# The order of two GpSimd remainders in the attention stage of a fused attention and mixture-of-experts kernel

## The chip, the cores and the metric

The kernel runs on one core of a Trainium2 chip. The metric is the device time of one execution in microseconds (us). The engines have the names of the profile: PE is TensorE's matrix multiply and PEld its weight load, DVE is VectorE, ACT is ScalarE, POOL is GpSimd, SP is SyncE, which here only issues DMAs. "SPq" is SP's queue of DMA issues.

## The reference, cut to what matters

```python
# attention: batch 4, 8 heads, 576 positions, head width 64, all float32
scores = scale * np.matmul(q, k.transpose(0, 1, 3, 2))          # scale = 1/8
cum = np.cumsum(np.log(np.clip(f, 0.0001, 1.0)), axis=-1)
scores = np.where(causal, -1e9, scores + cum[:, :, :, None] - cum[:, :, None, :])
attn = softmax(scores)                                          # over the last axis
x = np.matmul(attn, v)                                          # -> (2304, 512)
# then a layer of 8 experts (top 1, 512 -> 1024 -> 512), then a maxout layer of
# three 512x768 products and a 768x512 output product
```

The change touches only how q and k are prepared for the product of q and k.

## The kernel before, in words

Attention comes first and takes the first 222 us or so of the span; the routing and the experts follow, and then the shared layer. The 32 heads are worked on as 16 pairs of heads (p = 0 to 15, head h = 2p or 2p + 1), four pairs to a batch.

The product of q and k is made with matrix multiplies on a rounded 32-bit type (fp32r), so each operand is split in two: a high part, which is the operand cast to fp32r, and a low part, the remainder operand minus high part. For each pair there are four steps in `split_tasks(p)`:

- `q_hi` casts q into the tile At (128 partitions x 1152 elements, by DVE at L433 or by ACT at L435, both in the helper `evict`), and `k_hi` casts k into R1 the same way. The profile calls R1 and R2 both "R".
- `q_lo` (L321) computes the remainder of q on GpSimd, 64 x 1152 elements, into the other half of At; `k_lo` (L324) does the same for k, into R2.
- `q_copy` (L327) is a DMA that SP issues: it copies the cast q into the tile Bt.
- `load_pair` (L251) loads q and k of a pair as four DMAs, first two for q, then two for k, and `load_decay` (L262) loads two rows of the decay. Both are issued by SP. The raw q and k have two buffers each, so the load of pair p + 2 has to wait until all four steps of pair p have read theirs. At, Bt, R1 and R2 have three buffers.

A score task (L344) of a head multiplies At by R1 and Bt by R2 into a PSUM buffer "s" (three of them). DVE then takes the negated and masked maximum out of it (L361, tile P and its maximum nm), which frees the buffer; ACT takes the exponential (L381); PE transposes the result (L393 to L401, tiles t and tl), DVE or ACT copies it into PT (L433, L435), PE multiplies by v (L459, po), DVE or ACT copies that out (ot), PE turns it back (L478, pb), DVE scales it into XL (L487), and SP stores it (L498). At the end of a batch DVE does the routing of the batch's tokens (`route_batch`, with L550, L686 and L724 among its operands and steps).

The order of the instructions on each engine is fixed when the kernel is built, by a planner (`Sched`). A task has a list of engines that may do it, a planned cost for each, a number that says how urgent it is (smaller is earlier), and tasks that it waits for. The planner keeps a clock for each engine, takes again and again the open task that can start first (among equals the more urgent), gives it to the engine on which it would end first, with a handicap of 0.15 us for DVE and 2.0 us for GpSimd, and adds 0.2 us (`HOP`) where the task it waits for was on another engine. The tasks of pair p have the number 10 p - 6; the softmax tasks of head h have numbers from 5 h on. The planner knows of no case in which one engine slows another.

Of the kernel before, what the change touches and what calls it, by code (L numbers as in the profile page):

```python
# [214 lines left out]
def attention(tc, g, qT, kT, v, x_dram, es):  # L215
# [30 lines left out]
    def load_pair(p):  # L246
        q2 = ld.tile([128, 2, S], F32, tag="q2", name=f"q2_{p}")
        k2 = ld.tile([128, 2, S], F32, tag="k2", name=f"k2_{p}")
        for t, src in ((q2, qT), (k2, kT)):
            for r in range(2):  # L250
                nc.sync.dma_start(out=t[64 * r:64 * r + 64], in_=src[p])  # L251
        raws[p] = q2, k2
# [7 lines left out]
    def load_decay(p):  # L260
        for r, c in enumerate((g.chi, g.clo)):
            nc.sync.dma_start(out=R2[p % NQ][64 + r:65 + r].bitcast(F32).rearrange("p r s -> p (r s)"),  # L262
                              in_=c[2 * p:2 * p + 2, :].bitcast(F32))
# [28 lines left out]
    sd = Sched({"s": 3, "P": NPB, "t": 2, "tl": 1, "o": 2, "ot": 2}, 11.0)  # L292
# [11 lines left out]
    def split_tasks(p):  # L304
        i, u = p % NQ, 10 * p - 6
        load = None
        if p > 1:
            old = [fs[h, t, k] for h in (2 * p - 6, 2 * p - 5) for t in range(NBLK) for k in range(1 + (t == 4))] if p >= NQ else []
            load = sd.task("SP", 3.3, lambda e: load_pair(p), u - 8, ready[p - 2], lat=2.0)
            dec = sd.task("SP", 1.3, lambda e: load_decay(p), u - 4, old, lat=2.0)  # L310
        else:
            old, dec = [], None

        def q_hi(e):
            evict(e, At[i], raws[p][0])

        def k_hi(e):
            evict(e, R1[i], raws[p][1])

        def q_lo(e):  # L320
            nc.gpsimd.tensor_tensor(out=At[i][64:128], in0=raws[p][0][64:128], in1=At[i][64:128].bitcast(F32), op=ALU.subtract)  # L321

        def k_lo(e):
            nc.gpsimd.tensor_tensor(out=R2[i][0:64], in0=raws[p][1][0:64], in1=R1[i][0:64].bitcast(F32), op=ALU.subtract)  # L324

        def q_copy(e):
            nc.sync.dma_start(out=Bt[i][0:64].bitcast(F32), in_=At[i][0:64].bitcast(F32))  # L327

        qh = sd.task(("ACT", "DVE"), (1.02, 0.67), q_hi, u, old + [load])
        ql = sd.task("Pool", 2.6, q_lo, u, [qh])  # L330
        qc = sd.task("SP", 0.9, q_copy, u, [qh], lat=2.0)
        kh = sd.task(("ACT", "DVE"), (1.02, 0.67), k_hi, u, old + [load])
        kl = sd.task("Pool", 2.6, k_lo, u, [kh])
        ready[p] = [x for x in (qh, ql, qc, kh, kl, dec) if x is not None]

    def s_task(h, t, k, j0, w):
# [94 lines left out]
    def evict(e, out, in_):  # L431
        if e == "DVE":
            nc.vector.tensor_copy(out, in_)  # L433
        else:
            nc.scalar.activation(out=out, in_=in_, func=AF.Copy)  # L435
# [71 lines left out]

    last = [None]
    split_tasks(1)
    for p in range(NP):  # L510
        b, hp = divmod(p, NPAIR)
        if p + 2 < NP:
            split_tasks(p + 2) if p + 2 > 1 else None
        if hp == 1 and b + 1 < B:
            vdep[b + 1] = sd.task("SP", 3.3, lambda e, b=b: load_v(b + 1), 40 * b + 20, [fo[NPAIR * b - 1, u] for u in range(2)] if b else [], lat=2.0)
        head(2 * p)
        head(2 * p + 1)
        pair_out(p)
        if hp == NPAIR - 1:
            batch_out(b)  # L520
# [939 lines left out]
```

## Time and profile before

| what | value |
|---|---|
| median of 3 runs | 785.78 us (785.52 to 785.88) |
| the profiled execution | 785.06 us, of which its span 783.3 us and 1.76 us around it |
| mean granted clock of TensorE | 0.984 of full speed |
| PE busy | 738.9 us, 94% of the span |
| DVE busy | 461.9 us, 59% |
| ACT busy | 368.2 us, 47% |
| POOL busy | 237.7 us, 30% |

A share of busy time is a mean over stages with different limits; the change lies in the attention stage alone, so its stretches are what is to be read. An instruction that is held up after it has begun counts as busy for all of that time. A wait is put down to what was released last by the record, and "issue" is time in which the record shows nothing that was waited for.

### The profile page before, as it was taken

The page shows a single profiled execution, that of the slowest core. Times are in us where ns is not written, and L with a number is a line of the kernel's source. Part 1 is how long each engine was busy: PE and PEld are TensorE (multiplying, and loading weights), DVE is VectorE, ACT ScalarE, POOL GpSimd, SP SyncE. Part 2 cuts the span into 40 slices and gives each one's busy share as a digit, 9 for nine tenths or more (in the row PEclk, how much of TensorE's full clock was granted, in tenths as well). Part 3 has the DMA queues.
Part 4 walks back from the last instruction along what each step waited for, and adds up shares of the span by engine and source line. Part 5 has one row for each costly group of instructions (what it writes and reads, how often), then busy time and mean ns, then how long its engine had stood idle before and what let it go on. Part 6 is the DMA issues. An engine that isn't in the chain of part 4 may idle for free.

```text
span 783.3 us, 13403 instructions
## 1 busy us (share of the span) xinstructions
PE 738.9 (94%) x4862; PEld 682.3 (87%) x4862; DVE 461.9 (59%) x1076; ACT 368.2 (47%) x870; POOL 237.7 (30%) x189
## 2 busy tenths in 40 slices
PE   2989999999949998999999999999999999999996
PEld 1868877778738998999999999989999899999995
DVE  6888887988567998867767877941211211112110
ACT  5668887978836653454554563231211212212111
POOL 7464443532020344234223113341221211212112
PEclk9999999999978999999999999999999999999998
DMA  9959775751145465556474653200000000100001
GB/s 228 239 125 216 191 178 143 182 118 40 23 116 208 151 220 181 186 181 233 151 257 147 230 198 126 82 28 14 1 40 1 28 14 1 41 0 15 28 1 43
DMA packets 44614, 90.19 MB, mean 115 GB/s; under 512 B 23320, under 2 KB 23320, under 8 KB 44544
## 3 DMA queue, kind: packets, MB, share of 16 engines
q1 hardware_dynamic: 40960, 77.83, 34.0%
q0 software_dynamic: 3152, 9.88, 3.5%
q10 hardware_dynamic: 432, 1.57, 0.5%
q8 instruction: 40, 0.66, 0.3%
q14 instruction: 30, 0.25, 0.1%
HBM read 74.97 MB, written 9.44 MB: 108 GB/s over the span
## 4 chain that ended last, share of the span: by engine, by line
PE 75%; DVE 9%; DMA 7%; issue 4%; ACT 1%; POOL 1%; SPq 1%; POOLq 0%; DVEq 0%; ACTq 0%
PE pm L907 10%; PE pm L906 10%; PE pm L908 10%; PE s L344 6%; PE po L459 6%; PE t L397 4%; PE ph L908 3%; PE ph L907 3%; PE py L906 3%; PE py L908 3%; PE ph L906 3%; PE py L907 3%; PE po L1268 3%; PE po L1267 3%; PE po L1266 3%
## 5 line engine op out<-in xcount | busy, mean ns | idle before, releaser
L1240 DVE TENSOR_TENSOR tm<-pm,tm 128x384 f32<-128x384 f32 x72 | 40.1, 557 | 199.4 <-PE pm L908 198.2
L907 PE MATMUL pm<-x_y,m 128*128 128x384 f32 x432 | 144.5, 335 | 0.0
L908 PE MATMUL pm<-x_y,m 128*128 128x384 f32 x432 | 144.4, 334 | 0.0
L906 PE MATMUL pm<-x_y,m 128*128 128x384 f32 x432 | 144.4, 334 | 0.0
L381 ACT ACTIVATE P<-P,nm 128x576 f32<-128x576 f32 (+4 forms) x160 | 88.3, 555 | 17.0 <-DVE nm L361 16.7
L344 PE MATMUL s<-R,At 128*128 128x192 f32 (+1 forms) x192 | 71.3, 380 | 14.9 <-DVE At L271 10.5
L934 ACT ACTIVATE w<-stg 128x1024 fp32r<-128x1024 f32 x63 | 66.2, 1056 | 33.3 <-DMA stg<-in_w_dram 14.4
L907 PEld LDWEIGHTS pm<-x_y,m 128*128 128x128 f32 x432 | 81.1, 188 | 0.6 <-POOL x_y L1199 0.3
L951 DVE TENSOR_TENSOR w<-stg,w 128x1024 fp32r<-128x1024 f32 x54 | 70.2, 1304 | 19.3 <-ACT w L934 18.9
L907 PE MATMUL ph<-x,w 128*128 128x384 f32 (+7 forms) x256 | 79.3, 310 | 2.1 <-DVE x L1083 2.1
L906 PEld LDWEIGHTS pm<-x_y,m 128*128 128x128 f32 x432 | 81.1, 188 | 0.2
L908 PEld LDWEIGHTS pm<-x_y,m 128*128 128x128 f32 x432 | 81.1, 188 | 0.0
L906 PE MATMUL py<-h,w 128*128 128x384 f32 (+7 forms) x256 | 79.5, 311 | 0.8 <-DVE h L1141 0.8
L908 PE MATMUL ph<-x,w 128*128 128x384 f32 (+7 forms) x256 | 79.4, 310 | 0.8 <-DVE w L951 0.7
L906 PE MATMUL ph<-x,w 128*128 128x384 f32 (+7 forms) x256 | 79.4, 310 | 0.7 <-ACT x L934 0.7
L1251 POOL TENSOR_TENSOR g<-tm,g 128x384 fp32r<-128x384 f32 x34 | 36.5, 1074 | 141.4 <-ACT g L934 141.4
L908 PE MATMUL py<-h,w 128*128 128x384 f32 (+7 forms) x256 | 78.5, 307 | 0.4 <-DVE w L951 0.4
L907 PE MATMUL py<-h,w 128*128 128x384 f32 (+7 forms) x256 | 78.2, 305 | 0.0
L934 ACT ACTIVATE g<-tm 128x384 fp32r<-128x384 f32 x36 | 18.8, 524 | 115.9 <-DVE tm L1240 115.9
L361 DVE CUSTOM_DVE_ANT_0 P<-s,mask 128x288 f32<-128x288 f32 (+4 forms) x160 | 64.4, 422 | 11.1 <-PE s L344 6.7
L344 PE MATMUL s<-R,Bt 66*128 66x192 f32 (+1 forms) x192 | 60.2, 320 | 4.3 <-DMA R<-clo 4.3
L321 POOL TENSOR_TENSOR At<-q,At 64x1152 fp32r<-64x1152 f32 x15 | 40.3, 2684 | 77.1 <-DVE At L433 24.7
(246 smaller groups left out, 1620.4 us busy)
## 6 DMA issues: line engine op xcount, KB each, us to landing
stg<-in_w_dram SPq DMA_DIRECT2D x61, 512.0 KB
q<-in_q_dram SPq DMA_DIRECT2D x32, 288.0 KB
k<-in_k_dram SPq DMA_DIRECT2D x32, 288.0 KB
sd<-in_m_dram SPq DMA_DIRECT2D x18, 512.0 KB
Bt<-At SPq DMA_DIRECT2D x16, 288.0 KB
v<-in_v_dram SPq DMA_DIRECT2D x4, 1024.0 KB
x_dram<-XL SPq DMA_DIRECT2D x64, 64.0 KB
sd_o<-in_mo_dram SPq DMA_DIRECT2D x6, 512.0 KB
```

Source lines behind the costliest of these rows:

```text
L321: nc.gpsimd.tensor_tensor(out=At[i][64:128], in0=raws[p][0][64:128], in1=At[i][64:128].bitcast(F32), op=ALU.subtract)
L344: nc.tensor.matmul(st[:, 0:wp], lt[0:kk, r, ROW0[t]:ROW0[t] + 128], rt[0:kk, r, j0:j0 + wp], start=(ps_i == 0), stop=(ps_i == 1))
L361: nc.vector.tensor_tensor_reduce(out=P[0:n, j0:j0 + w], in0=st_.pop((h, t, k))[0:n, 0:w], in1=g.mask[0:n, m0:m0 + w], scale=-0.125, scalar ...
L381: nc.scalar.activation(out=P[0:n, 0:ext], in_=P[0:n, 0:ext], func=AF.Exp, bias=nm[0:n, k:k + 1], scale=-1.0, accum_out=sums[b][0:n, t, h % ...
L459: nc.tensor.matmul(po[64 * r:64 * r + 64, lo - c0:w], vt[b][0:n, a, (2 * hp + r) * D:(2 * hp + r + 1) * D], PT[(2 * p + r) % NPT][0:n, a, ...
L906: nc.tensor.matmul(out, whi, xhi, start=start, stop=False)
L907: nc.tensor.matmul(out, whi, xlo, start=False, stop=False)
L908: nc.tensor.matmul(out, wlo, xhi, start=False, stop=stop)
L934: nc.scalar.activation(out=out, in_=in_, func=AF.Copy)
L951: ENG[e].tensor_tensor(out=w[:, 1], in0=t, in1=w[:, 0].bitcast(F32), op=ALU.subtract)
L1240: nc.vector.tensor_tensor(out=mx[0], in0=mx["p", w][:, 0:MC], in1=mx[0], op=ALU.max)
L1251: ENG[e].tensor_tensor(out=ht[:, 1, :], in0=mx[0], in1=ht[:, 0, :].bitcast(F32), op=ALU.subtract)
```

## The change

In the kernel before, the cast of k does not depend on that of q, the remainder of q is given to GpSimd when the cast of q is done, and the remainder of k when the cast of k is done. After the change the cast of k depends on the cast of q, the remainder of k depends on the cast of k as before, and the remainder of q depends on the cast of q and on the remainder of k. So GpSimd gets the remainder of k first. The planned costs of the cast of k go from 1.02 to 1.1 us on ACT and from 0.67 to 0.8 us on DVE. The list `ready[p]`, which the score tasks and the load of pair p + 2 wait for, holds the same tasks.

```diff
         qh = sd.task(("ACT", "DVE"), (1.02, 0.67), q_hi, u, old + [load])
-        ql = sd.task("Pool", 2.6, q_lo, u, [qh])
         qc = sd.task("SP", 0.9, q_copy, u, [qh], lat=2.0)
-        kh = sd.task(("ACT", "DVE"), (1.02, 0.67), k_hi, u, old + [load])
+        kh = sd.task(("ACT", "DVE"), (1.1, 0.8), k_hi, u, old + [load, qh])
         kl = sd.task("Pool", 2.6, k_lo, u, [kh])
+        ql = sd.task("Pool", 2.6, q_lo, u, [qh, kl])
         ready[p] = [x for x in (qh, ql, qc, kh, kl, dec) if x is not None]
```

Pair 0 is split by code outside the planner (`first_split`) that the change leaves alone, so 15 pairs are affected.

## Rows read from the trace of the kernel before

**Rows 1.** The page's first part: busy time, share of the span and instructions.

```profile
PE 738.9 (94%) x4862; PEld 682.3 (87%) x4862; DVE 461.9 (59%) x1076; ACT 368.2 (47%) x870; POOL 237.7 (30%) x189
```

**Rows 2.** Stretches: length; busy PE, PEld, DVE, ACT, POOL; PE clock, DMA share, GB/s.

```profile
45.20:47.60 2.40, 0.02 (x2) 0.00 (x1) 2.40 (x6) 0.16 (x1) 1.65 (x2) 1.00 0.15 32
47.60:51.10 3.50, 3.50 (x15) 2.77 (x15) 2.35 (x11) 2.01 (x5) 3.42 (x2) 0.51 1.01 248
51.10:104.00 52.90, 52.90 (x439) 43.40 (x438) 45.66 (x157) 45.77 (x149) 24.47 (x10) 1.00 0.77 185
104.00:118.00 14.00, 12.32 (x97) 9.58 (x96) 12.32 (x40) 11.06 (x39) 6.21 (x4) 1.00 0.89 196
```

**Rows 3.** PE's timeline, idle places (one like 105.16 left out): in brackets idle time, releaser.

```profile
47.60 0.46 PE L344 MATMUL s<-R,At 128*128 128x192 f32 x1 [2.38 <-DVE nm L361]
...
105.16 0.41 PE L344 MATMUL s<-R,At 128*128 128x320 f32 x1 [0.84 <-DVE nm L361]
...
117.73 1.00 PE L478 MATMUL pb<-w,ot 128*128 128x144 f32 x6 [0.83 <-DVE ot L433]
...
167.37 1.00 PE L478 MATMUL pb<-w,ot 128*128 128x144 f32 x6 [0.87 <-DVE ot L433]
```

**Rows 4.** The chain that ended last, 97 to 118 us: start, length, what.

```profile
103.23 1.66 issue
...
115.01 1.96 DVE R L433
```

**Rows 5.** DVE's groups of instructions, 16 to 222 us: busy, mean ns, idle before.

```profile
L433 DVE CAST R<-k 128x1152 fp32r<-128x1152 f32 x13 | 26.5, 2036 | 0.0
...
L433 DVE CAST At<-q 128x1152 fp32r<-128x1152 f32 x12 | 10.9, 911 | 0.0
...
L724 DVE TENSOR_TENSOR ohp<-iota,rm 128x640 f16<-128x640 f32 x3 | 2.5, 826 | 0.0
```

**Rows 6.** DVE's timeline, single instructions: start, length.

```profile
29.60 0.64 DVE L550 TENSOR_TENSOR tri<-ioe,iok 128x64 f32<-128x64 f32 x1
...
40.25 2.50 DVE L433 CAST R<-k 128x1152 fp32r<-128x1152 f32 x1
...
43.51 2.63 DVE L433 CAST At<-q 128x1152 fp32r<-128x1152 f32 x1
46.06 0.75 DVE L433 CAST R<-k 128x1152 fp32r<-128x1152 f32 x1
...
101.89 3.07 DVE L433 CAST R<-k 128x1152 fp32r<-128x1152 f32 x1
...
125.92 0.76 DVE L433 CAST At<-q 128x1152 fp32r<-128x1152 f32 x1
```

**Rows 7.** POOL's timeline, single instructions: start, length, idle before.

```profile
27.53 2.64 POOL L321 TENSOR_TENSOR At<-q,At 64x1152 fp32r<-64x1152 f32 x1 [4.46 <-issue]
30.24 2.64 POOL L324 TENSOR_TENSOR R<-k,R 64x1152 fp32r<-64x1152 f32 x1
39.50 2.63 POOL L321 TENSOR_TENSOR At<-q,At 64x1152 fp32r<-64x1152 f32 x1 [6.62 <-DVE nm L361]
42.89 2.63 POOL L324 TENSOR_TENSOR R<-k,R 64x1152 fp32r<-64x1152 f32 x1 [0.75 <-DVE R L433]
46.27 3.04 POOL L321 TENSOR_TENSOR At<-q,At 64x1152 fp32r<-64x1152 f32 x1 [0.75 <-issue]
...
101.71 2.64 POOL L321 TENSOR_TENSOR At<-q,At 64x1152 fp32r<-64x1152 f32 x1 [2.42 <-DVE At L433]
```

**Rows 8.** The instructions of tile At: duration ns min/median/max, first and last start.

```profile
L435 ACT ACTIVATE At<-q x3: 1154/1156/1163, 11.4 to 142.2; 128x1152 fp32r<-128x1152 f32 x3
```

**Rows 9.** PE's timeline: the first score matmul of pair 2.

```profile
36.84 0.30 PE L344 MATMUL s<-R,At 128*128 128x288 f32 x1
```

**Rows 10.** SP's timeline: the four load issues of one pair.

```profile
104.38 1.11 SPq L251 DMA_DIRECT2D q<-in_q_dram  x2
107.76 1.10 SPq L251 DMA_DIRECT2D k<-in_k_dram  x2
```

## The prediction

> **What bounds the kernel now.** I read the page's first part, then the stretches of the attention stage, then the idle places of PE and the chain through them, and last the timelines of DVE and POOL side by side. The page says that PE is busy for 94% of the span [rows 1]. In the attention stage it is the bound almost without a break: in the stretch from 51.1 to 104.0 us it is busy for all of the 52.9 us, while DVE has 45.66 and ACT 45.77 us of work [rows 2]. So what a change here is worth is what it does to the moments in which PE stands still. From 30 us to the end of the score matmuls there are five: 2.38 us before 47.60, and 0.84, 0.83, 0.84 and 0.87 us (the third of these, before 154.79, repeats that before 105.16 to the hundredth) [rows 3]. Together they are 5.76 us. The first costs more than its length: PE was granted its full clock up to it, and in the 3.5 us behind it the clock was 0.51 of full speed, the lower of its two levels [rows 2]. At full speed that work would have taken 3.5 x 0.51 = 1.79 us, so 1.71 us more were lost. After the shorter gaps the clock did not fall: the stretch that holds those at 105.16 and 117.73 shows 1.00 [rows 2]. All five therefore cost 5.76 + 1.71 = 7.47 us.
>
> The releaser of each gap is DVE [rows 3]: nm of the softmax's first step, or the copy ot. What made DVE late is the instruction in front of these. The chain has the cast of k for 1.96 us just ahead of the gap at 117.73 [rows 4]. Ahead of 105.16 it has 1.66 us of "issue" [rows 4], which is a hole in the record of waits and not a cause: DVE's timeline shows a cast of k from 101.89 to 104.96 there [rows 6]. In front of the first gap stand two such casts in a row, 2.50 us from 40.25 and 2.63 us from 43.51 [rows 6].
>
> Those casts are held up. A cast that is left alone takes 0.75 us (the one at 46.06 [rows 6]). The 13 casts of k on DVE took 26.5 us where 13 x 0.75 = 9.75 would do, and the 12 of q took 10.9 where 9.0 would do [rows 5], so 16.7 + 1.9 = 18.6 us of DVE's time are lost. Put beside POOL, each long one ends some 0.6 us after a POOL subtraction ends. The cast at 40.25 ends at 42.75, the subtraction that began at 39.50 ends at 42.13; the cast at 43.51 ends at 46.14, the subtraction that began at 42.89 ends at 45.52; the one at 101.89 ends at 104.96, the subtraction that began at 101.71 ends at 104.35 [rows 6, 7]. So DVE's cast stands still while POOL subtracts. The Trainium skill says the same in "SBUF — State Buffer", section "Who interferes with whom": the two engines share one pair of ports, whoever starts first has it for its whole instruction, and casts are among the operations that need it. That rule also speaks against part of the change, and I come back to it among the rivals.
>
> **The change part by part.** The remainder of q may no longer start on the cast of q; POOL's first subtraction of a pair now waits for the cast of k, and that waits for the cast of q. So neither cast can meet a subtraction of its own pair. Ten or so casts of k were held by their own pair's `q_lo`, and all of the 16.7 us belongs to them; the 1.9 us belong to one cast of q, that at 43.51, which was held by the `k_lo` of the pair before.
>
> *The four later gaps.* Each stands behind one cast of k held by its own pair (3.07 us at 101.89, excess 2.3; the others have the same pattern). The excess is larger than the gap, so the gap goes whole: 0.84 + 0.83 + 0.84 + 0.87 = 3.38 us. A gap that went only in part would leave something between 0 and 3.38; I take the whole, as DVE has 52.9 - 45.66 = 7 us of slack in 53 us even with its stalls [rows 2].
>
> *The first gap.* The cast of k at 40.25 loses its stall of 2.50 - 0.75 = 1.75 us and ends near 41.0. Then POOL takes the remainder of k until 41.0 + 2.63 = 43.6 and that of q until 46.3. The cast of q of the next pair comes 1.75 us earlier, at 41.8, and still meets POOL. Its cost has two bounds, and nothing at all if the planner's new order puts it elsewhere. If it slips in between the two subtractions it is held to 43.6, 1.8 us, as long as now (1.88). If POOL's second subtraction goes first, it is held to 46.3, 1.8 + 2.63 = 4.4 us, against 3.63 us for both stalls now: 0.8 us worse. No row shows who wins when a cast waits at the seam of two subtractions. The nearest is the cast of k at 46.06, right behind a cast of q: it took 0.75 us, and the subtraction that began beside it at 46.27 ran long, 3.04 in place of 2.63 us [rows 6, 7], so a subtraction does give way to a cast. I take the middle: DVE is 1.75 us less late, the gap shrinks from 2.38 to 0.63 us, shorter than those after which the clock held, so the 1.71 us come back as well: 1.75 + 1.71 = 3.46 us. The bounds are 2.38 + 1.71 = 4.09 gained and 0.8 lost.
>
> *The new waits.* The cast of k behind that of q costs nothing on DVE, which takes them in turn anyway. Where the cast of q is on ACT (3 of 15, 1.156 us each [rows 8]) the cast of k starts up to 1.2 us later. POOL starts a pair's block at the end of the second cast and not of the first, but loses the wait between its two subtractions (0.75 us at 42.89 [rows 7]), so the block ends within about a microsecond of where it did. What waits for the block is the pair's first score matmul. It is nearest for pair 2, where `k_lo` ends at 30.24 + 2.64 = 32.88 and the scores begin at 36.84 [rows 7, 9]. There the cast of k was done by 30.24 at the latest, so the new block ends by 30.24 + 2 x 2.64 = 35.5: hidden by 1.3 us even so. If that cover went, each microsecond would be one of PE.
>
> The load of pair p + 2 starts with q, whose buffer now comes free last. SP issued q at 104.38 and had to wait to 107.76 for k [rows 10]; now it would issue q at about 107.8 and k at 108.9, 1.1 us later, with the stores of XL, the decay rows and `q_copy` queued behind. The cast that needs this load, two pairs on, begins at 125.92 [rows 6], 18 us after the k load was issued, so I cost it at nothing; what would uncover it is a load slower than some 17 us, and then it is the 1.1 us.
>
> *The planned costs* of 0.8 and 1.1 us change only the order. They move the choice between DVE and ACT by 0.05 us; the dependency moves it by 0.2 us towards the engine that did the cast of q, mostly DVE (12 of 15 [rows 5, 8]).
>
> Sum: 3.38 + 3.46 = 6.8 us off the profiled 785.06, so 778.3 us. The median of the runs is 0.72 us above that execution, so 779.0 us. What follows the attention is a separate plan and moves as a block.
>
> **The rivals.**
>
> *The pair 3 to 4 collision is not relieved.* POOL now has its two subtractions back to back, and if the second takes the port first, the first gap gives nothing or loses 0.8 us: 3.38 - 0.8 = 2.6 to 3.4 us gained, 782.4 to 783.2 us. For it speaks that the seam is untried; against it that POOL gave way at 46.06.
>
> *Other DVE work is held instead.* The operation at L550, 64 elements wide, ran from 29.60 to 30.24, to the end of the subtraction that began at 27.53 [rows 6, 7]: it was held too. The routing has a chain of such operations; today they are free of it (L724, ten times as wide, takes 826 ns [rows 5]). If the moved blocks meet two batches' routing, each loses up to one subtraction, 2.6 us, of which PE feels between 0.8 and 2.4 by the gaps in [rows 3]: 1.7 to 4.8 us back, 780.7 to 783.8 us. The Trainium skill has this rule as well ("SBUF — State Buffer", "Who interferes with whom"): a DVE instruction with two inputs in SBUF meets a GpSimd instruction that reads SBUF at the shared port. By that rule the row at L550 is one more case of the hold, and the trace agrees.
>
> *The new order gives it back.* The planner is greedy; a shift of 0.1 us can give the copies and exponentials another engine. PE's 7.5 us could come back as other gaps: 784.3 to 787 us. Against it: outside the casts nothing made PE wait.
>
> *Slower: the cast of k goes to ACT.* There it takes 1.156 us and delays an exponential; ACT is already at 45.77 of 52.9 us. If all 13 moved and each opened a gap of 0.84 us, 10.9 us are lost, net 4.1: 789.9 us. It decides from 6.8 / 13 = 0.52 us a cast. Against it: the 0.2 us for changing engine.
>
> *Slower: pair 2 comes late*, if its cast of k is put off beyond 31.6 us, with a cold clock behind the gap: 6.8 us would need a block over 4 us late, 786 to 789 us.
>
> **How the numbers follow.** The forecast has 0.57, the collision 0.14, the routing 0.06, the given back 0.11, ACT 0.08, pair 2 0.04. Within 0.2%, 1.6 us, a measurement of this kernel hardly tells a difference from none; that is 784.2 to 787.4 us. Faster: 0.57 + 0.14 + 0.06 = 0.77; same 0.11; slower 0.12. The forecast's own range is 777.8 (all 7.5 us and half a microsecond of spread) to 780.7. For 8 in 10 the range takes in the collision, the routing and the edge of the given back: 777.5 to 785.0.
>
> **What would show it.** Right: casts of k on DVE near 0.75 us, their group near 10 us in place of 26.5; no PE gap at the four later places; no stretch near 0.5 clock around 48 us; `k_lo` ahead of `q_lo` on POOL, back to back. Wrong: casts still over 2 us with POOL busy, which would name the collision; new waits of PE for P or PT behind ACT; PE waiting for R or At at a pair's first score.

## The result, and the profile after

The changed kernel takes 777.32 us (median of 4 runs, 776.84 to 778.65) against 785.83 us (4 runs, 785.52 to 786.92): a ratio of 0.990, with a 95% interval of 0.9879 to 0.9921. That is 8.5 us, where 6.8 were forecast. The median lies 0.2 us below the low end of the range.

The profiled execution took 778.65 us, the slowest of the four. Its first part of the page, against [rows 1]:

```profile
PE 736.6 (95%) x4862; PEld 681.6 (88%) x4862; DVE 443.4 (57%) x1075; ACT 369.3 (48%) x871; POOL 237.5 (31%) x189
```

DVE lost 461.9 - 443.4 = 18.5 us of work, and PE hardly any. Of DVE's 18.5 us the kernel gained less than half, because only what PE had waited for counts. The stretches of the changed kernel (columns as in [rows 2]):

```profile
45.00:52.00 7.00, 7.00 (x58) 5.86 (x56) 6.22 (x26) 6.56 (x24) 3.75 (x3) 1.00 0.70 168
52.00:104.00 52.00, 52.00 (x431) 42.23 (x431) 40.48 (x161) 45.23 (x142) 27.16 (x11) 1.00 0.81 196
104.00:118.00 14.00, 14.00 (x115) 11.54 (x113) 10.29 (x41) 11.62 (x40) 6.60 (x3) 1.00 0.67 154
```

Where [rows 2] had an empty PE and then a clock of 0.51, PE is now busy for all of 45 to 52 us at a clock of 1.00, and in 104 to 118 us for 14.00 of 14 us instead of 12.32. From 30 us to the last score matmul one idle place of over 0.3 us is left, and DVE has no part in it. PE's timeline has it, where [rows 3] had five:

```profile
38.73 0.55 PE L397 MATMUL t<-ident,P 128*128 128x128 f32 x3 [0.37 <-ACT PT L435]
```

DVE's casts, by group (16 to 222 us, as [rows 5]); the last line is from the view of the tile R and gives the casts of k on ACT (ns min/median/max):

```profile
L433 DVE CAST At<-q 128x1152 fp32r<-128x1152 f32 x12 | 9.0, 754 | 0.0
...
L433 DVE CAST R<-k 128x1152 fp32r<-128x1152 f32 x10 | 7.4, 736 | 0.0
...
L435 ACT ACTIVATE R<-k x5: 1150/1157/1162, 14.2 to 146.3; 128x1152 fp32r<-128x1152 f32 x5
```

No cast on DVE is held any more: 736 and 754 ns stand where 2036 and 911 stood. Three casts of k have moved to ACT. How pairs 3 and 4 miss each other is seen in DVE's timeline and, in the second fence, POOL's; they answer to [rows 6] and [rows 7]:

```profile
36.56 0.76 DVE L433 CAST At<-q 128x1152 fp32r<-128x1152 f32 x1
...
39.27 0.75 DVE L433 CAST R<-k 128x1152 fp32r<-128x1152 f32 x1
...
46.46 0.75 DVE L433 CAST At<-q 128x1152 fp32r<-128x1152 f32 x1
...
47.82 0.75 DVE L433 CAST R<-k 128x1152 fp32r<-128x1152 f32 x1
```

```profile
28.50 2.65 POOL L324 TENSOR_TENSOR R<-k,R 64x1152 fp32r<-64x1152 f32 x1 [5.07 <-DVE R L433]
31.21 2.64 POOL L321 TENSOR_TENSOR At<-q,At 64x1152 fp32r<-64x1152 f32 x1
40.15 2.63 POOL L324 TENSOR_TENSOR R<-k,R 64x1152 fp32r<-64x1152 f32 x1 [6.30 <-DVE rs L445]
42.86 2.66 POOL L321 TENSOR_TENSOR At<-q,At 64x1152 fp32r<-64x1152 f32 x1
48.70 2.65 POOL L324 TENSOR_TENSOR R<-k,R 64x1152 fp32r<-64x1152 f32 x1 [3.18 <-PE t L397]
```

Pair 3's block on POOL ends at 42.86 + 2.66 = 45.52, and the next cast of q begins at 46.46, 0.94 us later. So the collision of pairs 3 and 4 is not made smaller; it is gone. In DVE's order of instructions the cast of q of pair 4 stands 4 places behind the cast of k of pair 3 in the kernel before, and 19 places behind it after the change.

What the time is worth, place by place, comes from the start of a pair's first score matmul in both traces:

| pair | before | after | lead |
|---|---|---|---|
| 5 | 75.21 | 70.95 | 4.26 |
| 8 (behind the gap at 105.16) | 111.79 | 106.61 | 5.18 |
| 9 (behind 117.73) | 124.81 | 118.47 | 6.34 |
| 12 (behind 154.79) | 161.42 | 154.14 | 7.28 |
| 13 (behind 167.37) | 174.45 | 166.01 | 8.44 |
| 15 | 199.65 | 191.21 | 8.44 |

Pair 6 has the lead of pair 5, so from pair 5 on the lead rises only at the places that the prediction named (pairs 7 and 11, with 3.06 and 5.14 us, begin at another place in PE's new order and are left out). The first gap gave 4.26 us and the four later ones 4.18 us together. The attention ends 8.45 us earlier (215.46 against 223.91 us, at the matmul of L595), as much as the medians differ. The two profiled executions differ by only 785.06 - 778.65 = 6.4 us, because the one after lost 2 us again behind the attention: 561.3 against 559.4 us from that matmul to the end of the span. There PE's gap before 303.99 us lasted 2.14 us, where the same place before had 1.68, and the 4 us behind it had a clock of 0.58, where before had 1.00. In a second trace of the changed kernel (changed_again) the clock stays at 1.00 there and the part behind the attention takes 559.6 us.

The four later gaps gave more than their idle time of 3.38 us. The reason shows in PE's rows around 117.73 us before, and at the same place after:

```profile
116.59 0.31 PE L344 MATMUL s<-R,Bt 66*128 66x320 f32 x1
...
118.67 2.10 PE L459 MATMUL po<-PT,v 128*64 128x256 f32 x20
```

```profile
111.35 0.32 PE L344 MATMUL s<-R,Bt 66*128 66x320 f32 x1
111.50 0.90 PE L478 MATMUL pb<-w,ot 128*128 128x144 f32 x6
112.33 2.10 PE L459 MATMUL po<-PT,v 128*64 128x256 f32 x20
```

From the score matmul to the product with v it was 118.67 - 116.59 = 2.08 us and is 112.33 - 111.35 = 0.98 us, so a gap shown as 0.83 us cost 1.10. In an unbroken run the next matmul starts 0.15 us after one whose record lasts 0.32 us; in front of a gap the whole record counts as busy. The pb group behind the gap took 1.00 us instead of 0.90 as well.

### The profile page after: what moved, and what is told of

It reads as the page before. It is cut to its first block, busy times and chain, and to the rows that moved or that the text cites. A ratio compares the mean times of both kernels' runs of the same rounds, so it can differ in the third digit from the quotient of the medians.

```text
span 776.8 us, 13376 instructions
## 1 busy us (share of the span) xinstructions
PE 736.6 (95%) x4862; PEld 681.6 (88%) x4862; DVE 443.4 (57%) x1075; ACT 369.3 (48%) x871; POOL 237.5 (31%) x189
## 4 chain that ended last, share of the span: by engine, by line
PE 84%; DVE 7%; DMA 4%; ACT 2%; issue 2%; POOL 0%; SPq 0%; POOLq 0%; DVEq 0%; ACTq 0%
PE pm L907 10%; PE pm L908 10%; PE pm L906 10%; PE s L344 8%; PE po L459 6%; PE t L397 5%; PE ph L908 4%; PE ph L907 4%; PE ph L906 4%; PE py L906 3%; PE py L908 3%; PE py L907 3%; PE po L1268 3%; PE po L1267 3%; PE po L1266 3%; PE pb L478 2%
## 5 line engine op out<-in xcount | busy, mean ns | idle before, releaser
L324 POOL TENSOR_TENSOR R<-k,R 64x1152 fp32r<-64x1152 f32 x15 | 39.6, 2638 | 77.3 <-PE s L344 23.1
```

## The experiments

In the short diffs q_sub stands for the one GpSimd instruction of `q_lo`, and k_sub for that of `k_lo`. Each kernel is compared with the kernel before, measured beside it on the same chip (medians of the before: 785.53, 786.07 and 785.87 us in the three sets). "Order" is the order of the instructions that the planner fixed.

| run | us | ratio (95%) | casts of k on DVE, us each |
|---|---|---|---|
| old_plan_pool_swapped | 786.86 | 1.0018 (0.9996 to 1.0040) | 13 x 0.924 |
| new_plan_pool_as_before | 793.66 | 1.0093 (1.0062 to 1.0123) | 10 x 2.324 |
| casts_chained_only | 791.37 | 1.0070 (1.0045 to 1.0095) | 11 x 2.245 |
| half_remainder_of_q | 781.14 | 0.9936 (0.9907 to 0.9964) | 13 x 1.094 |
| swap_from_pair_5 | 781.11 | 0.9953 (0.9934 to 0.9971) | 13 x 0.877 |
| old_plan_swapped_pair_4_on_act | 779.99 | 0.9927 (0.9905 to 0.9950) | 12 x 0.736 |
| k_first_without_chain | 777.37 | 0.9910 (0.9879 to 0.9941) | 13 x 0.742 |
| new_order_old_costs | 777.60 | 0.9905 (0.9869 to 0.9941) | 13 x 0.734 |
| costs_only | 780.91 | 0.9942 (0.9921 to 0.9962) | 13 x 1.620 |
| k_cast_on_act_only | 786.89 | 1.0015 (0.9998 to 1.0032) | none |

**The swap alone, in the old order.** The order on PE, DVE, ACT and SP is that of the kernel before; only POOL's two subtractions change places.

```diff
         def q_lo(e):
-            q_sub
+            pass
         def k_lo(e):
-            k_sub
+            k_sub; q_sub
```

> Every engine but POOL keeps the order of the kernel before; on POOL the remainder of k is emitted first and that of q right behind it. If the casts held up by POOL are the whole cause, the 13 casts of k on DVE fall from 26.5 us to about 10, the four later gaps of PE go, and the time is 778 to 779 us if the cast of q near 42 us gets in between two subtractions, or 781 to 783 us if the second subtraction goes first. If the planner's new order of the other engines is the cause, the time stays at 785 to 786 us although the casts are short.

It gained nothing. The four later gaps are gone, as the prediction had it, but the first one has grown. DVE's timeline, POOL's, PE's idle place, and the stretch behind it:

```profile
43.33 2.63 DVE L433 CAST At<-q 128x1152 fp32r<-128x1152 f32 x1
45.88 3.17 DVE L433 CAST R<-k 128x1152 fp32r<-128x1152 f32 x1
```

```profile
42.71 2.63 POOL L324 TENSOR_TENSOR R<-k,R 64x1152 fp32r<-64x1152 f32 x1 [7.78 <-DVE R L433]
45.42 3.02 POOL L324 TENSOR_TENSOR At<-q,At 64x1152 fp32r<-64x1152 f32 x1
```

```profile
49.84 0.53 PE L344 MATMUL s<-R,At 128*128 128x192 f32 x1 [3.03 <-DVE nm L361]
```

```profile
49.84:57.84 8.00, 8.00 (x32) 6.81 (x32) 4.39 (x20) 4.83 (x16) 4.61 (x2) 0.50 0.78 183
```

This is the seam on which the prediction had no row. The waiting cast of q got in between the two subtractions: it ended at 45.96, 0.62 us after the first one's end at 45.34. The second subtraction ran 3.02 in place of 2.63 us, and then the next cast of k was held by it, to 49.05. So two casts in a row take 2.63 and 3.17 us, and PE stood for 3.03 us with 8 us at half clock behind it, and the 2 us after these had 0.70: 3.03 + 4.0 + 0.6 = 7.6 us, where the first gap of before cost 4.09. The 3.5 us lost there and a new gap of 0.53 us at 33.21 ate what the four later gaps gave.

**The new order, with POOL as before.** The counterpart: the changed kernel's order on PE, DVE, ACT and SP, with q_sub issued right behind the cast of q.

```diff
         def q_hi(e):
-            evict(e, At[i], raws[p][0])
+            evict(e, At[i], raws[p][0]); q_sub
         def q_lo(e):
-            q_sub
+            pass
```

> Every engine but POOL keeps the order of the changed kernel; on POOL the remainder of q is emitted with the cast of q, so it starts when that cast ends, as in the kernel before. If held casts are the cause, casts of k on DVE that do not follow the cast of q at once are held again (the group of 10 back to 15 us or more in place of 7.4), gaps of PE come back and the time is 781 to 787 us. If the new order is the cause, the time stays at 777 to 778 us.

Slower than the kernel before by 0.9%: the new order is worth nothing by itself. The subtraction of q still meets the casts of k (10 casts of 2.324 us on the mean, so held for 1.6 us), and PE has idle places of 1.40, 1.81, 1.55, 1.80 and 1.56 us at 52.52, 99.40, 121.30, 152.44 and 175.91 us. Between this kernel and the changed one, on the same order, lies only who goes first on POOL: 793.66 against 777.32 us.

**The chain of casts alone.**

```diff
-        kh = sd.task(("ACT", "DVE"), (1.02, 0.67), k_hi, u, old + [load])
+        kh = sd.task(("ACT", "DVE"), (1.1, 0.8), k_hi, u, old + [load, qh])
```

> The cast of k waits for that of q with the new planned costs, but POOL starts the remainder of q on the cast of q, as before. By the theory of held casts the chain alone is not the point: where the planner puts anything between the two casts the cast of k is held, so the group of casts of k stays above 18 us and the time is 783 to 787 us. If the chain of casts and the new costs make the gain by their order, it is 777 to 779 us.

Slower, by more than expected, and in the same way: 11 casts of k of 2.245 us on the mean, with gaps of 1.81, 1.55, 1.80 and 1.56 us in place of the four of 0.83 to 0.87, and some 3.4 us at half clock behind each. The first gap is smaller here, 0.94 us at 46.44, with one of 0.84 at 31.48.

**Half the remainder of q**, with the order of the kernel before. The kernel leaves out the remainder of the other 288 columns of each head.

```diff
-    q_sub over [64:128]
+    q_sub over [64:128, :, 0:288]
```

> The kernel before with the remainder of q computed for only half of the columns (288 of 576 of each head), the other half left out; the order on every engine is that of the kernel before. POOL's first subtraction then takes about 1.3 us in place of 2.64. If held casts are the cause, the casts of k fall by up to 1.3 us each, to a group of about 13 us, the four later gaps of PE go and the time is 778 to 781 us. If the order is the cause, the time stays at 785 to 786 us.

The subtraction took 1.41 us and the casts of k 1.094 us on the mean, so the length of the hold follows the length of what holds. The four later gaps are gone, though this order of events has two others (1.69 us at 20.55 and 0.78 at 34.49). The first gap stays, at 1.16 us, because the cast of q of pair 4 is held by the whole remainder of k of pair 3, which was not shortened (2.65 us from 46.70, beside the subtraction from 46.08), and this time the clock stayed at 1.00. Behind the gap of 0.78 us it did not; the last section shows that row.

**The swap from pair 5 on**, so that pairs 1 to 4 stay as they were.

```diff
         def q_lo(e):
-            q_sub
+            q_sub, only for p < 5
         def k_lo(e):
-            k_sub
+            k_sub; for p >= 5 also q_sub
```

> The kernel before in order on every engine; POOL takes the remainder of k first only from pair 5 on. The four later gaps lie there, the first gap does not. If each long cast behind a gap is the cause of that gap, the four later gaps go, 4 us or a little more are gained (781 to 782 us), and the first gap and the low clock behind it stay as in the kernel before. If the new order of the other engines makes the gain, nothing changes: 785 to 786 us.

781.11 us, as expected. PE's first gap is there unchanged (2.38 us at 47.68, with 3.4 us at half clock behind it), and no other is left; the attention ends at 219.89, 4.0 us earlier than before. That prices the four later gaps by themselves: 4.0 us, against 4.18 from the table of starts and 3.38 forecast.

**The swap in the old order, with pair 4's casts on ACT**, so that no cast of DVE is near the seam.

```diff
     old_plan_pool_swapped, and in q_hi and k_hi:
-            evict(e, ...)
+            evict("ACT" if p == 4 else e, ...)
```

> As old_plan_pool_swapped, but the two casts of pair 4, which there met the subtractions of pair 3 and were held twice, are done by ACT, which was held in no trace. If that double hold is what ate the gain there, the wide gap of PE near 47 us and the low clock behind it go, and the time is 777 to 780 us (two casts of 1.16 us more on ACT may cost up to 1 us). If the old order of the other engines is the cause, the time stays at 785 us or more.

779.99 us, against 786.86 with the two casts on DVE. The casts on DVE are 0.736 and 0.756 us on the mean, the first place has a gap of 1.29 us of another make (ot comes late behind a cast of k on ACT), and the clock stayed at 1.00. So the seam of pairs 3 and 4 is what had eaten the swap's gain, and not something that the swap does elsewhere.

**K first, without the chain of casts and with the old costs.**

```diff
-        ql = sd.task("Pool", 2.6, q_lo, u, [qh])
...
         kl = sd.task("Pool", 2.6, k_lo, u, [kh])
+        ql = sd.task("Pool", 2.6, q_lo, u, [qh, kl])
```

> The remainder of q waits for that of k, but the cast of k does not wait for that of q, and its planned costs are the old ones. In DVE's order the cast of q of pair 4 stands 18 instructions behind the cast of k of pair 3 (19 in the changed kernel, 4 in the kernel before), so it should miss the subtractions of pair 3. By the theory of held casts the chain of the two casts is then not needed: 776 to 779 us. If the chain is needed: 781 us or more.

777.37 us, the changed kernel's time. The planner, told of the new dependency alone, again moves the cast of q of pair 4, to 18 places behind the cast of k of pair 3. So the new dependency of the remainder of q alone gives the change's time. Two casts of q are still held in this trace, that of pair 4 (1.13 us from 45.27, up to the end of POOL's block) and that of pair 6 (2.03 us from 62.61), and yet PE has no idle place over 0.3 us from 16 us to the last score matmul: a held cast costs only where PE runs out of work behind it.

**The new dependencies, with the old costs.**

```diff
-        kh = sd.task(("ACT", "DVE"), (1.1, 0.8), k_hi, u, old + [load, qh])
+        kh = sd.task(("ACT", "DVE"), (1.02, 0.67), k_hi, u, old + [load, qh])
```

> The changed kernel with the old planned costs of the cast of k. The cast of q of pair 4 stands 18 instructions behind the cast of k of pair 3. If the costs only shuffle the order a little, 776 to 779 us, as the changed kernel. If the costs are what keeps the casts clear of POOL: 781 us or more, with casts of q or k over 2 us.

777.60 us, not told apart from the changed kernel. Its trace holds the rival of the other DVE work, though. DVE's timeline, POOL's and PE's:

```profile
31.02 2.65 DVE L550 TENSOR_TENSOR tri<-ioe,iok 128x64 f32<-128x64 f32 x1
```

```profile
30.96 2.63 POOL L321 TENSOR_TENSOR At<-q,At 64x1152 fp32r<-64x1152 f32 x1
```

```profile
34.60 0.40 PE L344 MATMUL s<-R,At 128*128 128x288 f32 x1 [2.14 <-DVE nm L361]
```

The operation at L550, 0.22 us where it is free (in k_first_without_chain), is held for the whole of the remainder of q, and PE stands for 2.14 us. Its attention ends at 217.24, 1.8 us later than the changed kernel's; with an interval some 5.7 us wide the medians do not show that.

**The costs alone.**

```diff
-        kh = sd.task(("ACT", "DVE"), (1.02, 0.67), k_hi, u, old + [load])
+        kh = sd.task(("ACT", "DVE"), (1.1, 0.8), k_hi, u, old + [load])
```

> The kernel before with the new planned costs of the cast of k alone. The casts of k still follow POOL's first subtraction, and the cast of q of pair 4 stands 8 instructions behind the cast of k of pair 3. By the theory of held casts nothing is gained: casts of k near 2 us, gaps of PE, 784 to 793 us. If the costs make the gain by their order: 777 to 780 us.

A miss: 780.91 us, 5 us faster than the kernel before, with the casts of k still long. DVE's group of them, one cast of k, and POOL's subtraction of the same pair:

```profile
L433 DVE CAST R<-k 128x1152 fp32r<-128x1152 f32 x13 | 21.1, 1620 | 1.0 <-DMA k<-in_k_dram 1.0
```

```profile
103.24 0.73 DVE L433 CAST R<-k 128x1152 fp32r<-128x1152 f32 x1
```

```profile
100.45 2.64 POOL L321 TENSOR_TENSOR At<-q,At 64x1152 fp32r<-64x1152 f32 x1 [3.59 <-DVE nm L361]
```

The planner now has other work between the two casts of this pair and of one other, so that the cast of k begins behind the subtraction's end at 103.09 and takes 0.73 us. At pairs 3 and 4 the stalls are shorter (2.34 and 1.95 us), and the gap of 2.38 us has become one of 0.93 at 46.66 with the clock at 1.00. In all, five gaps of 0.82 to 0.93 us are left. Planned costs changed by some 0.1 us thus moved 5 us, because two casts of k now begin too late to meet a subtraction; where they still meet one, they are held as before (2.0 to 2.5 us).

**The cast of k on ACT only**, the other way to get it out of POOL's way, and a test of the rival on ACT.

```diff
-        kh = sd.task(("ACT", "DVE"), (1.02, 0.67), k_hi, u, old + [load])
+        kh = sd.task("ACT", 1.02, k_hi, u, old + [load])
```

> The kernel before with every cast of k from pair 1 on given to ACT, the rest left to the planner. ACT was held in no trace, so by the theory of held casts the 16.7 us of held casts of k go and PE's later gaps with them: 777 to 782 us, one cast of q near 43 us still held. By the rival of the prediction, that 15 casts of 1.16 us are too much for ACT and open gaps of PE of their own, 787 to 792 us.

786.89 us, no gain: just below the rival's time and well above my own. By PE's waits ACT is not what took it back: from 16 us to the last score matmul DVE ends every wait of PE over 0.3 us. DVE's timeline in the routing of the first batch, then POOL's and PE's:

```profile
82.17 0.75 DVE L575 TENSOR_REDUCE L<-XL 128x40 f32<-128x320 f32 x1
...
83.18 1.15 DVE L581 TENSOR_TENSOR e<-L,lmax 128x40 f32<-128x40 f32 x1
84.36 2.65 DVE L583 TENSOR_TENSOR e<-e,w 128x40 f32<-128x40 f32 x1
...
96.10 2.45 DVE L623 TENSOR_TENSOR ohs<-ohs,o 128x8 f16<-128x8 f16 x1
```

```profile
81.04 3.22 POOL L324 TENSOR_TENSOR R<-k,R 64x1152 fp32r<-64x1152 f32 x1 [9.17 <-ACT R L435]
84.34 2.61 POOL L321 TENSOR_TENSOR At<-q,At 64x1152 fp32r<-64x1152 f32 x1
92.58 2.64 POOL L324 TENSOR_TENSOR R<-k,R 64x1152 fp32r<-64x1152 f32 x1 [5.63 <-ACT R L435]
95.93 2.61 POOL L321 TENSOR_TENSOR At<-q,At 64x1152 fp32r<-64x1152 f32 x1 [0.70 <-DVE At L433]
```

```profile
87.53 0.18 PE L595 MATMUL pr<-oh,tris 128*128 128x40 f16 x1 [3.09 <-DVE oh L589]
```

Two operations of 40 and 8 elements a partition, 0.20 and 0.17 us in the changed kernel's trace, took 2.65 and 2.45 us and ended within 0.1 us of POOL's ends at 86.95 and 98.54. PE stood for 3.09 us, and then for 1.94 more at 98.75, each time with a lower clock behind it (20 us from 84 on had a mean clock of 0.77). This is the rival "other DVE work is held instead", at the very routing that the prediction named, in a kernel that moved POOL's blocks there. The Trainium skill ("SBUF — State Buffer", section "Who interferes with whom") says that such a two-input operation meets a GpSimd read at the shared port, that a reduction does not, and that whoever issues first has the port. The trace agrees: L581 and L583 were held, while the reduction at L575 began and ended within POOL's 81.04 to 84.26 and took 0.75 us, as in the changed kernel (0.76).

**One more step: the setup copies at L104 on ACT**, in the changed kernel, beside the changed kernel once more.

```diff
-        nc.vector.tensor_copy(g.w144[s, :, r, 0:D], g.ident[s, s].unsqueeze(1).to_broadcast([64, NPAIR, D]))
+        nc.scalar.activation(out=g.w144[s, :, r, 0:D], in_=g.ident[s, s].unsqueeze(1).to_broadcast([64, NPAIR, D]), func=AF.Copy)
```

> The changed kernel with the two setup copies of line 104 (2.21 us together on DVE near 19 us, while POOL subtracts) done by ACT at the same place in the order. By the theory they are held too; without them DVE is 2.2 us earlier there and PE's short wait at 21.9 us goes: 0 to 1.5 us less than the changed kernel, since PE runs at its lower clock there anyway. If they are not held, no difference.

> The changed kernel once more, as the base for changed_setup_copies_on_act in the same runs: 776 to 779 us.

776.75 us (ratio 0.9881, 0.9860 to 0.9903) against 778.39 us for the changed kernel (0.9919, 0.9890 to 0.9948). PE's idle 0.17 us before 21.70 is gone and the attention ends 0.36 us earlier (214.98 against 215.34); the rest of the 1.6 us between the medians has no place in the traces, whose executions stand the other way round (777.86 against 776.71 us), and the intervals overlap. So it is inconclusive: at most a small step further. PE ran at its slower pace there, as expected: 0.33 us from the score matmul at 21.94 to the next in the changed kernel's trace, against 0.20 at 32.23, both of 192 columns.

## Why the prediction was right, and where its sizes were off

The direction and the mechanism came as forecast. The size was 1.7 us short, which puts the time just outside the range, and one of its two terms came out for another reason than the one given.

**What bounds it: right.** PE's idle places were the cost. With them gone the kernel is 8.5 us faster, and the other 10 of DVE's 18.5 freed microseconds changed nothing.

**The mechanism of the hold: shown.** Same order on PE, DVE, ACT and SP, subtractions exchanged: 786.86 against 785.53 us in the old order, 793.66 against 777.32 in the new; each time the casts of k fall from over 2 us to under 0.93. With the subtraction of q 1.2 us shorter in the old order, the casts of k are 0.94 us shorter on the mean.

**The four later gaps: right in kind, too small by 0.8 us.** Forecast 3.38, measured 4.18 by the starts and 4.0 by swap_from_pair_5. The term was the idle time as shown, and a gap costs 0.1 to 0.3 us more than it shows (1.10 for 0.83).

**The first gap: the step that was mis-sized.** I took the middle, 3.46 us, on the ground that a subtraction gives way to a cast at the seam. It does, but that does not help: old_plan_pool_swapped shows that the cast which gets in at the seam itself takes 2.63 us, and the cast behind it 3.17, where 0.75 would do. My bound of "0.8 us worse" was also too small (about 3.5), as the lower clock lasted 8 us there and more, and not 3.5. What made the term come out at 4.26, above my upper bound of 4.09, was the clause that I had put down as "nothing at all if the planner's new order puts it elsewhere": the new dependency moved the cast of q of pair 4 beyond POOL's block. That was luck: nothing in the planner aims at it, and on the old order the same swap made this gap longer. The two terms, 0.80 us each, are the whole of the 1.6 us by which the forecast gain was short.

**The new waits: nothing, as said.** Pair 2's block on POOL ended at 33.85 (forecast: by 35.5), and PE had no wait for At or R behind 30 us, so what [rows 8] and [rows 9] bounded stayed covered. The load of [rows 10] is that of pair 11, and it came later than forecast: q at 110.05 and k at 111.50 us, where the prediction had 107.8 and 108.9, although the attention around it ran 4 to 6 us earlier than before. SP issued the two with no wait in between, but the planner had put them behind the `q_copy` of the next pair:

```profile
109.41 0.54 SPq L327 DMA_DIRECT2D Bt<-At  x1
110.05 1.35 SPq L251 DMA_DIRECT2D q<-in_q_dram  x2
111.50 1.19 SPq L251 DMA_DIRECT2D k<-in_k_dram  x2
```

The cast of q that needs this load began at 119.58, so the 18 us of cover behind the k load shrank to 8. DVE had no wait for a load from 25 us on, so the term was still nothing, but with half the room that the prediction gave it.

The chain of waits, where [rows 4] had the cast of k, holds only PE's matmuls from 92 to 112 us; its summary by line of that stretch:

```profile
by line: PE s L344 38.4%; PE po L459 21.5%; PE t L397 20.3%; PE pb L478 8.0%; PE tl L399 6.0%; PE t L401 3.5%; PE tl L393 2.8%
```

**The planned costs: nothing that the medians show in the changed kernel** (new_order_old_costs), but not without effect by themselves (costs_only, 5 us faster). That they "change only the order" was true, and the price of an order was missed.

**The rivals.** The collision of pairs 3 and 4 was real in the old order, and it cost more than I gave it. The held DVE work came true in two experiments (2.14 and 3.09 us of PE) but not in the changed kernel, where L550 took 0.77 us and PE did not wait. The cast of k did go to ACT three times more, and no gap followed. Whether the planner would keep clear of the seam in another kernel is not known: it knows nothing of the hold.

## What to carry to other kernels

Where two engines block each other, put the short operation of the blocked one ahead of all the long ones of the other, and then look at the next block: long operations back to back leave a seam, and what waits there pulls its successor into the second one. Price a stall by the gap on the bound engine and the clock behind it, not by the stalls summed up. In a kernel with a planned order, test an edit on the old order as well as on its own, since half of an effect, or its sign, can come from the new order.

## What the runs showed of the hardware that was not expected

The length of a gap alone does not say whether PE's clock falls. After nearly all gaps up to 1.29 us in the attention stage of these traces it stayed at 1.00, but a gap of 0.78 us in half_remainder_of_q was followed by the lower level, and two gaps of 1.81 us went either way. PE's rows and the stretches behind them, first in half_remainder_of_q, then in new_plan_pool_as_before and in casts_chained_only:

```profile
34.49 0.41 PE L344 MATMUL s<-R,At 128*128 128x320 f32 x1 [0.78 <-DVE nm L361]
```

```profile
34.49:38.49 4.00, 4.00 (x20) 2.66 (x22) 2.91 (x13) 2.62 (x9) 0.00 (x0) 0.64 1.05 236
```

```profile
99.40 0.40 PE L344 MATMUL s<-R,At 128*128 128x288 f32 x1 [1.81 <-DVE nm L361]
```

```profile
99.40:103.40 4.00, 4.00 (x33) 3.27 (x33) 3.74 (x18) 3.66 (x11) 2.18 (x1) 1.00 0.87 182
```

```profile
94.99 0.48 PE L344 MATMUL s<-R,At 128*128 128x288 f32 x1 [1.81 <-DVE nm L361]
```

```profile
94.99:98.99 4.00, 4.00 (x21) 2.77 (x22) 2.13 (x11) 2.93 (x9) 2.17 (x1) 0.57 0.69 157
```

A gap of 1.40 us (at 52.52 in the former) was followed by half clock, and the one of 2.14 us in new_order_old_costs by full clock. Where the clock fell it took 3.5 to 6.5 us from the end of the gap to come back in most places, but 8.4 us after 1.40 and 9.2 after 3.03. So a gap of 0.8 to 2.4 us can have two prices, and by the times which one is paid seems to differ between executions of one kernel: the runs of new_plan_pool_as_before went from 787.59 us at a mean clock of 0.984 to 796.17 us at 0.974. What decides it, these runs do not tell. The prediction's step from a gap "shorter than those after which the clock held" to 1.71 us that come back was therefore not a safe one.
